# Four raw buffers for heads 0 to 7, loaded three heads ahead

## The chip, the cores and the metric

The kernel runs on one core of one Trainium2 chip. The time is that of one execution on the device, in microseconds (us); several runs are made and their median counts. A profile is one more execution, recorded instruction by instruction. Engines: TensorE (PE; its weight loads are PEld), VectorE (DVE), ScalarE (ACT), GpSimd (POOL), SyncE (SP). SP computes nothing here, it issues nearly all DMAs; a few are issued from ScalarE's queue (ACTq).

## The reference

Batch 4, 8 heads, 576 positions, head size 64; 32 heads in all. Weights come in float64.

```python
# attention, each of the 32 heads
cum = cumsum(maximum(s, 0))
scores = q @ k.T / 8 + minimum(-(cum[:, None] - cum[None, :]), 0)   # causal
attn = softmax(scores)                     # minus the row's maximum, sum + 1e-9
x = attn @ v                               # to [batch, 576, 512]
# first mixing
gate = sigmoid(causal_conv5(x, conv_w))
x = (gate * (x @ w_val)) @ w_out
# second mixing
u, v = split(relu(x @ w_in), 2)            # 512 columns each
v = layernorm(v)
out = (u * (w_spatial @ v + b_spatial)) @ w_out2
```

## The kernel before, in words

One loop goes over the heads, w = 0 to 32. Step w computes the scores of head w in five row tiles (of 64, 128, 128, 128 and 128 rows; the last in two pieces, so six pieces), and for head w-1 the transposes of the exponentials. VectorE reads each score piece out of PSUM, adds the mask and takes the row's extremum (line 233); ScalarE takes the exponential with its row sum (line 238); TensorE transposes (line 279), ScalarE copies the transposes to `pt` (line 281). Two heads make a pair: `normalise` takes the reciprocals of a pair's row sums, `lay_sums` stores them from ScalarE's queue into `r_d` in DRAM, `spread_sums` loads them back, spread over 64 partitions, as `R` in two halves (line 262). `pv` multiplies by v for a pair (line 303), and VectorE multiplies its result by `R` to `x` (lines 306 to 309). `conv` then makes the gate `z`.

The scores of heads 0 to 7 (NATIVE = 8) are plain float32 matmuls on the raw q and k tile (line 222); a row of ones and a row of `cum` in partition 64 bring in the bias. From head 8 on the raw tile is split by `prep` into a high and a low part (tiles `qk`, `kd`, `cn`), and a score piece is two faster matmuls (lines 224 and 225).

`load(h)` brings head h in: three DMAs into the raw tile, for heads 0 to 7 one more for the row of `cum` (from the tile for heads 0 and 1, from its copy `one_d` in DRAM for the others), and two into `vraw` (v, four buffers in turn). So a load is five or six issues on SP. There are two raw tiles, `RAW[0]` and `RAW[1]`; head h uses `RAW[h % 2]`, so the load of head h waits until the scores of head h-2 are done (heads 0 to 7), or its split (later ones). `vraw` of head h takes the buffer of head h-4 and waits for that head's `pv`. `qk` has two buffers as well, unused until head 8.

Beside the heads runs the work of a generator, a piece after each group of score tiles (`more`). In the first heads it converts float64 weights, chunk by chunk (`from_f64`): conv_w, four chunks of woT, four of w_in, four of w_val, four more of w_in, then w_out2. A chunk is one load on SP (line 382), one instruction on ScalarE (384), three on VectorE (385 to 387), two on GpSimd (390, 391), and a split in two. Then TensorE folds w_out into w_in (`fold`), and from step 9 on does the mixing of batch 0, later of the others, between the scores.

A scheduler orders the instructions of every engine by their place in the program and by when it expects operands and buffers. The orders are fixed when the kernel is built, and every engine, and SP's queue, works through its own in turn.

Of the kernel before, what the change touches and what calls it, by code (L numbers as in the profile page):

```python
# [8 lines left out]
F32R = mybir.dt.float32r  # L9
# [7 lines left out]
NATIVE = 8  # L17
# [7 lines left out]
def tile_stickbreak_attention_moe(  # L25
# [18 lines left out]
    NH, S = s.shape  # L44
# [20 lines left out]
    V, G, A, T, SY = nc.vector, nc.gpsimd, nc.scalar, nc.tensor, nc.sync  # L65

    def f(ap):
        return ap.bitcast(F32)
# [13 lines left out]
    early = ctx.enter_context(tc.tile_pool(name="early", bufs=1))  # L82
# [8 lines left out]
    RAW = [early.tile([128, 2, S], F32, name=f"raw{i}") for i in range(2)]  # L91
# [36 lines left out]
    for j in range(2):  # L128
        P.append(early.tile([128, PW], F32, name=f"p{j}"))
        G.memset(P[j][64:, 192:256], 0.0)  # L130
        G.memset(P[j][:, 576:640], 0.0)
    mid = ctx.enter_context(tc.tile_pool(name="mid", bufs=1))

    def tmp(name, dt=F32):
# [8 lines left out]
    raw, vraw, L = {}, {}, {}  # L143
# [4 lines left out]
    def load(h, cum=None):  # L148
        if h >= NH:
            return  # L150
        raw[h] = r = RAW[h % 2]
        n = 64 if h < NATIVE else 128
        src = qk2[h].rearrange("p (t s) -> p t s", t=2)[0:n, ::-1]
        by = r[0:n].rearrange("p t s -> p (t s)")
        SY.dma_start(by[:, 64:1088].rearrange("p (t s) -> p t s", t=2)[:, :, 0:448], src[:, :, 0:448])
        by = by.rearrange("p (g c) -> p g c", c=64)
        SY.dma_start(by[:, 0:17:16], src[:, :, 512:])
        SY.dma_start(by[:, 8:18:9], src[:, :, 448:512])
        if h < NATIVE:
            SY.dma_start(r[64:65, 0, :], one_d[h:h + 1] if cum is None else cum[h:h + 1])  # L160
        vraw[h] = early.tile([128, 6, D], F32, tag="vraw", name="vraw", bufs=4)
        vh = vp[h].rearrange("p (c d) -> p c d", c=5)
        SY.dma_start(vraw[h][:, 0:4], vh[:, 0:4])
        SY.dma_start(vraw[h][64:128, 4:], vh[0:64, 0::4])
# [78 lines left out]
    def normalise(p):  # L243

        d = early.tile([128, 2, 5], F32, tag="den", name="den", bufs=2)
        V.tensor_scalar_add(d, sm[p % 2], 1e-9)
        R[p] = early.tile([128, 2, 5], F32, tag="rin", name="rin", bufs=2)
        V.reciprocal(out=R[p], in_=d)
# [22 lines left out]
    def transposes(h, tiles):  # L271

        p = P[h % 2]
        if h not in PT:
            PT[h] = early.tile([128, PTW], F32, tag="pt", name="pt", bufs=2)
        for bank in tiles:
            pt = room("t", "pst", h)
            for t, (o, way) in enumerate(BANKS[bank]):
                T.transpose(pt[:, 128 * t:128 * t + 128], p[:, o:o + 128], ident[:, way:way + 128])  # L279
            to, o, n = PTO[bank]  # L280
            A.activation(PT[h][:, to:to + n], pt[:, o:o + n], AF.Copy)  # L281
# [3 lines left out]
    def pv(h):  # L285

        b, p = h // H, (h % H) // 2
        x = X[b, p] = early.tile([128, S], F32, tag=f"x{p}", name=f"x{p}", bufs=1)
        r = R.pop(h // 2)
        pts = [PT.pop(h + j) for j in range(2)]  # L290
        vs = [vraw.pop(h + j) for j in range(2)]
        po = ps.tile([128, 512], F32, tag="o", name="pso", bufs=1)
        pq = ps.tile([128, 512], F32, tag="q", name="psq", bufs=1)[:, 0:64]
        parts = [(0, 0, po), (2, 1024, po[:, 192:]), (3, 1408, po[:, 320:]), (4, 1344, po[:, 448:]),
                 (1, 576, po[:, 64:]), (5, 512, pq)]
        first = None
        for c, o, to in parts:
            k0 = 64 if c > 3 else 0
            for j in (1, 0):
                with ExitStack() as es:  # L300
                    if first is not None:
                        es.enter_context(tc.issue_after(first))
                    m = T.matmul(to[64 * j:64 * j + 64], vs[j][k0:, 4 + (c == 4) if c > 3 else c, :],  # L303
                                 pts[j][k0:, o:o + to.shape[1]], start=c in (0, 5), stop=c in (1, 5))
                first = first or m.ins
        V.tensor_tensor(out=x[:, 64:448], in0=po[:, 0:384], in1=r[:, 1:4].rearrange("p i q -> p (i q)"), op=ALU.mult)
        xs, ps4, r4 = [t.rearrange("p (g c) -> p g c", g=2) for t in (x[:, 448:], po[:, 384:], r[:, 4])]
        V.tensor_tensor(out=xs, in0=ps4, in1=r4[:, ::-1], op=ALU.mult)
        V.tensor_tensor(out=x[:, 0:64], in0=pq, in1=r[:, 0, 0:64], op=ALU.mult)
# [3 lines left out]
    def conv(b, p):  # L313
        x = X[b, p]
        if p == 0:
            Z[b] = early.tile([128, NP, S], F32, tag="z", name="z", bufs=1)
        z = Z[b][:, p, :]
        A.activation(z, x, AF.Copy, scale=cw[:, p, 4:5])  # L318
        for k in range(3, -1, -1):
            d = 4 - k  # L320
            V.scalar_tensor_tensor(out=z[:, d:], in0=x[:, :S - d], scalar=cw[:, p, k:k + 1], in1=z[:, d:],  # L321
                                   op0=ALU.mult, op1=ALU.add)
        A.activation(z, z, AF.Tanh)
# [16 lines left out]
    if NATIVE:  # L340
        load(0, cum)
        load(1, cum)
        SY.dma_start(one_d, cum[0:NATIVE])
    if not NATIVE:
        load(0)
        load(1)
# [164 lines left out]
    def mixing_a(b):  # L511

        xh, xl = [], []
        for p in KC:
            xh.append(mid.tile([128, S], F32R, tag=f"xvh{p}", name=f"xvh{p}"))
            xl.append(mid.tile([128, S], F32R, tag=f"xvl{p}", name=f"xvl{p}"))
            hi_of(A, xh[p], X[b, p])
            lo_of(V, xl[p], X[b, p], xh[p])
        z = Z[b]
        g = GT[b] = mid.tile([128, NP, 2 * S + 64], F32R, tag="g", name="g")  # L520
        gh, gl = g[:, :, 0:S], g[:, :, S + 64:]
        for mc in KC:
            wh, wl = weight_chunk(wv_d, mc, b)
            for hf in range(2):
                pt = ps.tile([128, 512], F32, tag="m", name="psm", bufs=2)
                three(pt[:, 0:HS], KC, lambda kc: (wh[:, kc, :], wl[:, kc, :]),
                      lambda kc: (xh[kc][:, hs[hf]], xl[kc][:, hs[hf]]))
                gated_split(gh[:, mc, hs[hf]], gl[:, mc, hs[hf]], pt[:, 0:HS], z[:, mc, hs[hf]], 1.0)
                yield 1.44
# [87 lines left out]
    def more(n):  # L617
        with tc.high_priority(offset=0):
            more_(n)
# [42 lines left out]
    def start():  # L662

        m = mixing_a(0)
        yield from both(m, first, 2)
        m = mixing_b(0)
        yield from both((next(m) for _ in range(5)), second_steps())
        for ec in range(4):
            fold(ec, 0)
            yield 2.56  # L670
        open_late()
        yield from both((next(m) for _ in range(8)), third_steps())
        yield from m
# [14 lines left out]
    for w in range(NH + 1):  # L688
        if w == H + 1:
            queue.clear()  # L690
            queue.append(start())
        elif w % H == 1 and w > 1 and w < NH:
            queue += [mixing_a(w // H - 1), mixing_b(w // H - 1)]
        if w >= NATIVE:
            load(w + 2)
        n_g = [3, 11.5, 10.0, 7.6, 6.0][0 if w <= H else 1 if w <= H + 4 else 2 if w <= 2 * H else 3 if w <= 3 * H else 4]
        gs = [n_g / 5] * 5
        if w < NH:
            scores(w, [0, 1])
        if w > H + 1 and w % 2:  # L700
            pv(w - 3)
            conv((w - 3) // H, ((w - 3) % H) // 2)
        if w > 0:
            transposes(w - 1, [3, 2])
        if w % 2 == 0 and w > 0:
            lay_sums(w // 2 - 1)
        more(gs[0])
        if w < NH:
            scores(w, [2])
        prep(w + 1)  # L710
        if 0 < w <= H:
            transposes(w - 1, [0])
        more(gs[1])
        if w < NH:
            scores(w, [3])
        if w > 0:
            transposes(w - 1, [0, 1] if w > H else [1])
        if w % 2 == 0 and w > 0:
            spread_sums(w // 2 - 1)
        more(gs[2])  # L720
        if w < NH:
            scores(w, [4])
            if w < NATIVE:
                load(w + 2)
            if w % 2:
                normalise(w // 2)
        more(gs[3])
        if w % 2 == 0 and (0 < w <= H or w == NH):
            pv(w - 2)
            conv((w - 2) // H, ((w - 2) % H) // 2)  # L730
        more(gs[4])
# [57 lines left out]
```

## Time and profile before

| | us |
|---|---|
| median of 3 runs | 505.13 |
| lowest, highest | 504.92, 505.87 |
| the profiled execution | 505.84 |
| its span, first to last instruction | 504.1 |
| TensorE busy in the span | 478.4 |
| VectorE, ScalarE, GpSimd busy | 320.0, 315.8, 166.6 |

The span is 1.7 us shorter than the time of the same execution, and that time is 0.7 us above the median. Busy shares of the span are averages over stages which differ, so the views below go by stretches of time.

### The profile page before, as it was taken

To read this page: it belongs to the slowest core of one execution; us is meant where nothing else is said; L and a number is where in the kernel's file an instruction comes from. 1 tells how busy PE (TensorE), PEld (TensorE's weight loads), DVE (VectorE), ACT (ScalarE), POOL (GpSimd) and SP (SyncE) were. 2 spreads that over 40 slices of the span, in tenths; PEclk is the share of its full clock that TensorE was granted. 3 is DMA by queue.
4 is the path that set the end of the run, shared out by engine and by line. 5 is a ranking of instruction groups with operands and counts; after the bars stand their busy time and mean duration, and the time that the engine had idled before them with its cause. 6 is when DMAs were issued, how large, how long until landed. Compare 5 with 4: busy or idle time off the path is not lost.

```text
span 504.1 us, 9144 instructions
## 1 busy us (share of the span) xinstructions
PE 478.4 (95%) x3138; PEld 402.7 (80%) x3138; DVE 320.0 (63%) x835; ACT 315.8 (63%) x796; POOL 166.6 (33%) x183
## 2 busy tenths in 40 slices
PE   8787889899899999998999999999999999999997
PEld 5443556678777899996969889898878979988997
DVE  5799999598989783742768366654885534124120
ACT  2887876787776875773667657585778524234322
POOL 5697252056583103101353013002243023136130
PEclk9999799989999999999999999999999999999999
DMA  3877466557493634377631413677611072700002
GB/s 92 255 232 241 133 209 223 156 159 236 122 270 121 185 106 123 99 212 191 186 87 42 130 39 85 187 217 200 169 37 32 0 262 53 225 1 2 0 11 85
DMA packets 51567, 68.23 MB, mean 135 GB/s; under 512 B 23936, under 2 KB 39456, under 8 KB 51520
## 3 DMA queue, kind: packets, MB, share of 16 engines
q1 hardware_dynamic: 46592, 62.84, 42.6%
q10 hardware_dynamic: 4928, 4.80, 2.8%
q8 instruction: 25, 0.41, 0.4%
q14 instruction: 22, 0.18, 0.1%
HBM read 54.91 MB, written 9.16 MB: 127 GB/s over the span
## 4 chain that ended last, share of the span: by engine, by line
PE 65%; DVE 17%; DMA 9%; ACT 3%; issue 3%; SPq 2%; POOL 1%; DVEq 0%; ACTq 0%; POOLq 0%
PE psm L426 12%; PE psm L428 11%; PE psm L427 11%; PE pso L303 6%; PE pst L279 5%; PE psm L594 4%; PE psm L596 3%; PE psm L595 3%; DVE p L233 3%; PE pss L224 3%; PE pss L225 3%; DVE z L321 3%; DMA raw<-in_qk 2%; DMA wv<-wv_d 2%; DMA R<-r_d 2%
## 5 line engine op out<-in xcount | busy, mean ns | idle before, releaser
L238 ACT ACTIVATE p<-p,nm 64x64 f32<-64x64 f32 (+4 forms) x160 | 88.5, 554 | 20.4 <-DVE nm L233 19.9
L233 DVE CUSTOM_DVE_ANT_0 p<-pss,mask 64x64 f32<-64x64 f32 (+4 forms) x160 | 62.8, 413 | 24.1 <-PE pss L225 18.4
L281 ACT ACTIVATE pt<-pst 128x512 f32<-128x512 f32 (+2 forms) x128 | 59.5, 496 | 21.4 <-PE pst L279 20.7
L279 PE MATMUL pst<-ident,p 128*128 128x128 f32 x416 | 64.5, 281 | 1.3 <-ACT p L238 1.2
L80 POOL TENSOR_TENSOR y<-gt,y 128x288 fp32r<-128x288 f32 x32 | 27.9, 872 | 106.6 <-ACT y L73 106.6
L80 POOL TENSOR_TENSOR g<-gt,g 128x288 fp32r<-128x288 f32 x32 | 28.2, 886 | 96.2 <-ACT g L73 96.0
L321 DVE SCALAR_TENSOR_TENSOR z<-x,cw,z 128x575 f32<-128x575 f32 (+1 forms) x64 | 56.1, 876 | 6.3 <-ACT z L318 5.8
L279 PEld LDWEIGHTS pst<-ident,p 128*128 128x128 f32 x416 | 50.7, 144 | 10.7 <-issue 3.4
L303 PE MATMUL pso<-pt,vraw 128*64 128x512 f32 (+4 forms) x320 | 52.6, 437 | 0.0
L224 PE MATMUL pss<-qk 128*64 128x64 f32 (+1 forms) x144 | 44.0, 324 | 3.3 <-DVE nm L233 3.0
L225 PE MATMUL pss<-kd,cn 66*64 66x64 f32 (+1 forms) x144 | 41.8, 296 | 0.0
L504 DVE TENSOR_TENSOR gt<-psm,u 128x288 f32<-128x288 f32 x32 | 14.5, 455 | 43.0 <-PE psm L598 33.3
L222 PE MATMUL pss<-raw 128*128 128x320 f32 (+4 forms) x96 | 31.8, 437 | 8.6 <-DVE nm L233 5.6
L426 PE MATMUL psm<-g,wch 128*128 128x288 f32 x128 | 38.7, 302 | 0.9 <-DVE wcl L80 0.9
L594 PE MATMUL psm<-wsh,vh 128*128 128x288 f32 x128 | 38.5, 304 | 0.4 <-DVE gt L504 0.4
L428 PE MATMUL psm<-g,wch 128*128 128x288 f32 x128 | 38.1, 297 | 0.0
L427 PE MATMUL psm<-g,wcl 128*128 128x288 f32 x128 | 38.0, 297 | 0.0
L596 PE MATMUL psm<-wsl,vh 128*128 128x288 f32 x128 | 37.5, 297 | 0.0
L595 PE MATMUL psm<-wsh,vl 128*128 128x288 f32 x128 | 37.3, 296 | 0.0
L303 PEld LDWEIGHTS pso<-pt,vraw 128*64 128x64 f32 (+1 forms) x320 | 19.0, 135 | 22.6 <-issue 15.4
L502 DVE SCALAR_TENSOR_TENSOR gt<-z,psm 128x288 f32<-128x288 f32 x32 | 14.2, 449 | 35.5 <-PE psm L428 35.4
L426 PE MATMUL psm<-xvh,wv 128*128 128x288 f32 x96 | 29.7, 309 | 2.9 <-DMA wv<-wv_d 2.4
(168 smaller groups left out, 1345.2 us busy)
## 6 DMA issues: line engine op xcount, KB each, us to landing
raw<-in_qk SPq DMA_DIRECT2D x24, 448.0 KB
wv<-wo_d SPq DMA_DIRECT2D x12, 512.0 KB
R<-r_d SPq DMA_DIRECT2D x32, 160.0 KB
wv<-wv_d SPq DMA_DIRECT2D x10, 512.0 KB
out<-ot ACTq DMA_DIRECT2D x32, 144.0 KB
vraw<-in_vp SPq DMA_DIRECT2D x32, 128.0 KB
cn<-qk SPq DMA_DIRECT2D x24, 144.0 KB
raw<-in_qk SPq DMA_DIRECT2D x48, 64.0 KB
```

The source lines that it names most:

```text
L224: T.matmul(pst[0:m, o:o + b - a], qa[:, q0:q0 + m], kb[:, k0 + a:k0 + b], start=True, stop=False)
L225: T.matmul(pst[0:m, o:o + b - a], qc[0:KD, q0:q0 + m], kd[0:KD, k0 + a:k0 + b], start=False, stop=True)
L233: LAST["V"] = V.tensor_tensor_reduce(out=row[:, a:b], in0=src, in1=mask[0:m, o:o + b - a], scale=-0.125, scalar=3.0e38 if a == 0 else nm[0 ...
L238: A.activation(row, row, AF.Exp, bias=nm[0:m, i:i + 1], scale=-1.0, accum_out=sm[h // 2 % 2][0:m, h % 2, i:i + 1])
L279: T.transpose(pt[:, 128 * t:128 * t + 128], p[:, o:o + 128], ident[:, way:way + 128])
L281: A.activation(PT[h][:, to:to + n], pt[:, o:o + n], AF.Copy)
L303: m = T.matmul(to[64 * j:64 * j + 64], vs[j][k0:, 4 + (c == 4) if c > 3 else c, :], pts[j][k0:, o:o + to.shape[1]], start=c in (0, 5), sto ...
L321: V.scalar_tensor_tensor(out=z[:, d:], in0=x[:, :S - d], scalar=cw[:, p, k:k + 1], in1=z[:, d:], op0=ALU.mult, op1=ALU.add)
L426: T.matmul(pt, ah, bh, start=j == 0, stop=False)
L427: T.matmul(pt, al, bh, start=False, stop=False)
L428: T.matmul(pt, ah, bl, start=False, stop=j == n - 1)
L594: T.matmul(o, vh[c][:, cs], wsh[:, c, hs[hf]], start=c == 0, stop=False)
```

## The change

Heads 0 to 7 now use four raw tiles in turn: the two old ones and two allocated under the tag `qk`, whose two buffers are later those of the split tiles. Their constant rows are set by GpSimd, two memsets for each. Head 2 is loaded ahead of the loop; in the loop step w loads head w+3 for w = 0 to 6, where it loaded head w+2 for w = 0 to 7. From head 10 on the loads stand as before. `vraw` still has four buffers.

```diff
--- before.py
+++ after.py
@@ -129,6 +129,11 @@
         P.append(early.tile([128, PW], F32, name=f"p{j}"))
         G.memset(P[j][64:, 192:256], 0.0)
         G.memset(P[j][:, 576:640], 0.0)
+    for i in range(2):
+        t = f(early.tile([128, 2, S], F32R, tag="qk", name="rawq", bufs=2))
+        G.memset(t[64:], 0.0)
+        G.memset(t[64:65, 1, :], 1.0)
+        RAW.append(t)
     mid = ctx.enter_context(tc.tile_pool(name="mid", bufs=1))
 
     def tmp(name, dt=F32):
@@ -148,7 +153,7 @@
     def load(h, cum=None):
         if h >= NH:
             return
-        raw[h] = r = RAW[h % 2]
+        raw[h] = r = RAW[h % (4 if h < NATIVE else 2)]
         n = 64 if h < NATIVE else 128
         src = qk2[h].rearrange("p (t s) -> p t s", t=2)[0:n, ::-1]
         by = r[0:n].rearrange("p t s -> p (t s)")
@@ -341,6 +346,7 @@
         load(0, cum)
         load(1, cum)
         SY.dma_start(one_d, cum[0:NATIVE])
+        load(2)
     if not NATIVE:
         load(0)
         load(1)
@@ -720,8 +726,8 @@
         more(gs[2])
         if w < NH:
             scores(w, [4])
-            if w < NATIVE:
-                load(w + 2)
+            if w + 1 < NATIVE:
+                load(w + 3)
             if w % 2:
                 normalise(w // 2)
         more(gs[3])
```

The lines below the edits move by 5, 6 further down (line 155 becomes 160, line 262 becomes 267, line 382 becomes 388).

The first place is SP's queue behind the loads of heads 0 and 1. `raw_66` and `raw_67` are the two old tiles, `rawq` the new ones. Before, from the store of one_d to the end of head 2's raw load:

```order
L343 DMA one_d<-cum 8x576
L347 DMA cum_d<-ch 32x576
L348 DMA cum_d<-cl 32x576
L382 DMA wg<-in_conv_w 128x40
L382 DMA wg<-in_woT 128x1024
L163 DMA vraw<-in_vp 128x256
L164 DMA vraw<-in_vp 64x2x64
L382 DMA wg<-in_woT 128x1024
L155 DMA raw_66<-in_qk 64x2x448
L157 DMA raw_66<-in_qk 64x2x64
L158 DMA raw_66<-in_qk 64x2x64
L160 DMA raw_66<-one_d 1x576
```

And with the change:

```order
L348 DMA one_d<-cum 8x576
L160 DMA rawq<-in_qk 64x2x448
L162 DMA rawq<-in_qk 64x2x64
L163 DMA rawq<-in_qk 64x2x64
L165 DMA rawq<-one_d 1x576
L168 DMA vraw<-in_vp 128x256
L169 DMA vraw<-in_vp 64x2x64
L353 DMA cum_d<-ch 32x576
L354 DMA cum_d<-cl 32x576
L388 DMA wg<-in_conv_w 128x40
L388 DMA wg<-in_woT 128x1024
L160 DMA rawq<-in_qk 64x2x448
```

Head 2's six issues have moved from behind conv_w and two woT chunks to right behind one_d; cum_d, conv_w and woT stand behind them, and head 3's raw load follows the first woT chunk.

The second place is SP's queue around R of pair 0. Before, from the last woT chunk; the raw load is head 4's:

```order
L382 DMA wr<-in_woT 128x1024
L382 DMA wg<-in_w_in 128x1024 x2
L180 DMA kd_117<-cum_d 2x576
L155 DMA raw_66<-in_qk 64x2x448
L157 DMA raw_66<-in_qk 64x2x64
L158 DMA raw_66<-in_qk 64x2x64
L160 DMA raw_66<-one_d 1x576
L382 DMA wg<-in_w_in 128x1024
L180 DMA kd_118<-cum_d 2x576
L382 DMA wr<-in_w_in 128x1024
L262 DMA R<-r_d 64x640 x2
L163 DMA vraw<-in_vp 128x256
```

And with the change, from the last woT chunk; the raw load is head 5's, the vraw loads are those of heads 4 and 5:

```order
L388 DMA wr<-in_woT 128x1024
L160 DMA raw_67<-in_qk 64x2x448
L162 DMA raw_67<-in_qk 64x2x64
L163 DMA raw_67<-in_qk 64x2x64
L165 DMA raw_67<-one_d 1x576
L267 DMA R<-r_d 64x640
L168 DMA vraw<-in_vp 128x256
L169 DMA vraw<-in_vp 64x2x64
L267 DMA R<-r_d 64x640
L168 DMA vraw<-in_vp 128x256
L169 DMA vraw<-in_vp 64x2x64
L388 DMA wg<-in_w_in 128x1024 x2
```

R stood in one piece behind the four w_in chunks and ahead of vraw; now the vraw load of head 4 stands between its halves and the w_in chunks behind both.

The third place is SP's queue around R of pair 1. Before; the raw load is head 6's:

```order
L382 DMA wg<-in_w_val 128x1024 x3
L155 DMA raw_66<-in_qk 64x2x448
L157 DMA raw_66<-in_qk 64x2x64
L262 DMA R<-r_d 64x640 x2
L158 DMA raw_66<-in_qk 64x2x64
L160 DMA raw_66<-one_d 1x576
L163 DMA vraw<-in_vp 128x256
L164 DMA vraw<-in_vp 64x2x64
L163 DMA vraw<-in_vp 128x256
L164 DMA vraw<-in_vp 64x2x64
```

And with the change; the raw load is head 8's, the vraw loads are those of heads 6 and 7:

```order
L388 DMA wr<-in_w_val 128x1024
L160 DMA raw_66<-in_qk 128x2x448
L162 DMA raw_66<-in_qk 128x2x64
L163 DMA raw_66<-in_qk 128x2x64
L185 DMA kd_117<-cum_d 2x576
L185 DMA kd_118<-cum_d 2x576
L168 DMA vraw<-in_vp 128x256
L169 DMA vraw<-in_vp 64x2x64
L267 DMA R<-r_d 64x640 x2
L168 DMA vraw<-in_vp 128x256
L169 DMA vraw<-in_vp 64x2x64
```

R of pair 1 stood ahead of both vraw loads; now it stands between them, behind that of head 6.

## Rows read from the trace of the kernel before

**Rows 1.** The page, part 1: busy us of each engine, share of the span, instructions.

```profile
PE 478.4 (95%) x3138; PEld 402.7 (80%) x3138; DVE 320.0 (63%) x835; ACT 315.8 (63%) x796; POOL 166.6 (33%) x183
```

**Rows 2.** Stretches (us): length, then busy us (instructions) by engine, granted clock, DMA share, GB/s.

```profile
8.00:25.00 17.00, 13.05 (x63) 8.26 (x64) 10.67 (x47) 12.19 (x39) 7.67 (x8) 1.00 0.75 208
25.00:85.00 60.00, 51.64 (x260) 32.13 (x261) 58.07 (x147) 46.42 (x117) 35.66 (x24) 0.94 0.68 215
85.00:100.00 15.00, 13.51 (x87) 9.90 (x85) 9.55 (x28) 11.81 (x33) 0.00 (x0) 1.00 0.54 147
100.00:137.50 37.50, 34.57 (x209) 28.93 (x210) 35.67 (x88) 29.11 (x74) 20.24 (x16) 0.95 0.56 170
137.50:504.10 366.60, 359.11 (x2505) 318.62 (x2503) 200.62 (x517) 214.26 (x535) 96.14 (x117) 1.00 0.40 116
```

**Rows 3.** TensorE's waits to 140 us: line, releaser, us in total, times, longest.

```profile
PE pss L222 <- DVE nm L233: 5.6, 7, 1.0
PE pss L224 <- DVE nm L233: 3.0, 2, 2.6
```

**Rows 4.** VectorE by line, 20 to 60 us: count, busy us, mean ns of one.

```profile
L387 DVE SCALAR_TENSOR_TENSOR wg<-wg 128x512 int32<-128x512 int32 x4 | 3.4, 861 | 0.0
L386 DVE TENSOR_SCALAR wg<-wg 128x512 int32<-128x512 int32 x5 | 3.4, 676 | 0.0
...
L385 DVE TENSOR_SCALAR wg<-wg 128x512 f32<-128x512 f32 x5 | 2.8, 561 | 0.0
```

**Rows 5.** SP's queue in order of time: start us, us of the issue, line.

```profile
10.70 0.32 SPq L347 DMA_DIRECT2D cum_d<-ch  x1
...
12.49 0.43 SPq L163 DMA_DIRECT2D vraw<-in_vp  x1
12.96 0.60 SPq L164 DMA_DIRECT2D vraw<-in_vp  x1
13.61 0.59 SPq L382 DMA_DIRECT2D wg<-in_woT  x1
14.30 0.60 SPq L155 DMA_DIRECT2D raw<-in_qk  x1
14.95 0.60 SPq L157 DMA_DIRECT2D raw<-in_qk  x1
15.59 0.61 SPq L158 DMA_DIRECT2D raw<-in_qk  x1
16.24 0.45 SPq L160 DMA_DIRECT2D raw<-one_d  x1
```

**Rows 6.** Timeline near the first loads: start us, us, work, [idle before and what ended it].

```profile
13.39 0.22 ACT L384 ACTIVATE wg<-wg 128x20 f32<-128x20 f32 x1 [2.46 <-DMA wg<-in_conv_w]
...
19.05 1.55 POOL L390 TENSOR_SCALAR wg<-wg 128x512 int32<-128x512 uint32 x1 [1.76 <-DMA wg<-in_woT]
...
20.37 0.82 PE L222 MATMUL pss<-raw 128*64 128x64 f32 x4 [2.33 <-DMA raw<-in_qk]
```

**Rows 7.** VectorE's waits from 8 to 140 us, columns as in rows 3.

```profile
DVE x L306 <- DMA R<-r_d: 3.0, 2, 2.2
DVE wg L385 <- ACT wg L384: 1.8, 1, 1.8
```

**Rows 8.** Timeline: sums of pair 0 stored, R loaded; R of pair 3, its use.

```profile
28.18 0.56 ACTq L256 DMA_DIRECT2D r_d<-rt  x1
...
33.04 1.12 SPq L262 DMA_DIRECT2D R<-r_d  x2
...
94.86 1.11 SPq L262 DMA_DIRECT2D R<-r_d  x2
...
99.04 0.56 DVE L306 TENSOR_TENSOR x<-pso,R 128x384 f32<-128x384 f32 x1 [2.22 <-DMA R<-r_d]
```

**Rows 9.** GpSimd by line to 9 us, columns as in rows 4.

```profile
L94 POOL MEMSET raw<- 64x1152 f32 x1 | 1.1, 1052 | 0.3 <-POOLq L774 0.3
```

**Rows 10.** One more stretch, columns as in rows 2.

```profile
101.00:105.00 4.00, 3.88 (x16) 3.34 (x17) 3.97 (x12) 3.96 (x12) 2.12 (x1) 0.58 0.17 37
```

## The prediction

> **What bounds the kernel now.** I read the page's busy shares first: TensorE is busy 478.4 of 504.1 us [rows 1], so the whole change can only play for the 26 us in which TensorE is idle, and for stretches in which its clock is low. The table by stage says where these lie [rows 2]. Behind 137.5 us TensorE is busy 359.1 of 366.6 us: nothing that loads heads 0 to 8 earlier shortens that stage. Between 8 and 137.5 us it is busy 112.8 of 129.5 us, so 16.7 us are idle there: 4.0 before 25 us, 8.4 from 25 to 85, 1.5 to 100 and 2.9 to 137.5.
>
> What ends these waits? Mostly VectorE: the score matmuls wait 5.6 us in seven pieces (heads 0 to 7) and 3.0 us in two (from head 8 on) until VectorE has read an earlier score tile [rows 3]. VectorE is the bound from 25 to 85 us, busy 58.07 of 60 us, because it converts the float64 weights between the score tiles. A weight chunk costs it three instructions of 0.56, 0.68 and 0.86 us, 2.1 us together [rows 4]. So in that stage a wait is worth something only if it is a wait of VectorE, and VectorE's own waits are few: 1.9 us. Before 25 us it idles 6.3 of 17 us and from 85 to 100 us 5.4 of 15 us [rows 2]. The change must earn its gain in these two places, and must not make a new wait in between.
>
> **The change part by part.** The arithmetic is the same; two pairs of memsets are new, no load is added, and the loads and everything else are put in another order.
>
> (a) *Head 2 no longer waits for head 0's buffer.* TensorE waits 2.33 us for its raw tile, whose first load is issued at 14.30 us [rows 5, 6]. Now it is issued right behind one_d, where cum_d stood, some 3.6 us earlier. Gain 2.3 us; bounds 0 (something else holds VectorE at that place) and 2.3.
>
> (b) *conv_w.* The load of head 2 is six issues (0.60, 0.60, 0.61, 0.45, 0.43 and 0.60 us, sum 3.3 us [rows 5]) put ahead of cum_d, conv_w and the first woT chunk. Now VectorE waits 1.8 us for conv_w's conversion [rows 7]; ScalarE begins that at 13.39 us, when the load has landed [rows 6]. Landing moves to 16.7 us. In the new order VectorE meets this conversion behind the fifth score tile of head 1 instead of behind the fifth of head 0, at about 16 us by the old times less the old wait. So 1.8 us go and about 0.6 come back: gain 1.2, bounds 0.9 and 1.8.
>
> (c) *woT later.* The second woT chunk was issued at 13.61 us and GpSimd began on it at 19.05 us, 5.4 us later [rows 5, 6]. Now head 2's load (3.3 us) and head 3's raw tile (0.60, 0.60, 0.61, 0.45: 2.3 us) stand ahead of it: issue 19.2, landing about 24.6 us. VectorE wants it behind the last tile of head 2, which with (a) and (b) gained it reaches at about 23.4 us. Loss 1.2 us; bounds 0 and 2.
>
> (d) *R of pair 0 behind a vraw load.* The vraw buffers are still four, so the load of head w+3 waits for pv of head w-1, an iteration earlier than before. On SP's queue the first vraw load of head 4 now stands between the two halves of R, and of head 5 right behind; the two w_in chunks that stood ahead of R now stand behind all of these. R's halves were issued at 33.04 us, 4.9 us after r_d [rows 8]. r_d moves up with head 2 by 1.5 to 2 us, so R's first half goes out at about 30 to 31.5 us; one half (0.56), two vraw issues (0.43 and 0.60) and the other half (0.56) end 2.2 us later; another pair of halves took 99.04 - 94.86 - 1.11 = 3.1 us from the last issue to the multiply that waited for it [rows 8]. R is there at 35.3 to 36.8 us. VectorE comes to the multiply (x, line 306) earlier than before, for two w_in chunks, 4.2 us [rows 4], are no longer ahead of it: at 32 to 33 us. It then stands for 2 to 4 us, and what is queued behind x on VectorE is the last tile of head 3, which TensorE's next score matmuls wait for. Loss 3 us; bounds 2 and 4.
>
> [...] In the trace SP's queue is served strictly in its order: no row of it starts before the one ahead [rows 5]. [...]
>
> (e) *R of pair 1* stands in the same way behind vraw of head 6 (before: ahead of it). VectorE is saturated there, so I take less: loss 1 us; bounds 0 and 2.7 (the 2.2 us that R's second half is held up in (d), and 0.5 for the last matmuls of pv, which I estimate).
>
> (f) *The memsets.* GpSimd gets two of 64x1152 (1.05 us each [rows 9]) and two of one row, which I take at no more than half a wide one each, ahead of its last masks: the masks come some 2 to 3 us later. They were done before the first score tile needs them; most is covered by that slack. Loss 0.3 us; bounds 0 and 0.5. Without that cover it would be the whole 3.2.
>
> (g) *Heads 8 to 10.* The raw tile of head 9 was issued behind w_val and pair 2; now it is loaded an iteration earlier, so the split of heads 9 and 10 is no longer late. [...] TensorE is otherwise full here, and the new order also puts mixing matmuls ahead of head 8's third tile, so a wait saved is kept. [...]
>
> Behind 137.5 us the order differs up to head 28, but TensorE has 7.5 us idle there in all; I take 0, with 1 us to either side.
>
> **The sum.** -2.3 - 1.2 + 1.2 + 3 + 1 + 0.3 - 3.5 = -1.5 us. The profiled execution took 505.84 us (span 504.1 and 1.7 around it), 0.7 above the median of 505.13. Against its own time that is 504.3, against the median **503.6 us**, 0.3% faster. With every bound at its best: -2.3 - 1.8 + 0 + 2 + 0 + 0 - 4.7 - 1 = -7.8; at its worst: 0 - 0.9 + 2 + 4 + 2.7 + 0.5 + 0 + 1 = +9.3.
>
> **The rivals.** What a measurement of this kernel can tell from no change is about 0.2%, 1.0 us.
>
> *Slower: SP's queue blocks.* R of pairs 0, 1 and 2 is stuck behind vraw loads that wait for pv, and the weight loads behind R with it. Place: x <- R on VectorE between 32 and 76 us. Price: 4 + 2.7 + 2 for pair 2 (as pair 3 before, 2.2), 8.7 us, against gains of 2.3 + 1.2 and losses of 1.2 + 0.3 in (b), (c), (f), and half of (g), 2.4: net +4.3, 509.4 at full price; it decides from about 5.5 us of such waits on (2.3 + 1.2 - 1.5 + 3.5, the point of no change) and counts as slower from 6.5. For it: the order, in which vraw stands ahead of R for both pairs. Against: pv(0) is issued early in head 3, so vraw may find it done. Chance 0.33; about 507 as its middle. [...]
>
> *No change.* VectorE's work up to head 8 is the same sum, and it has but 1.9 us idle from 25 to 85 us; heads that come earlier only trade places with weights that come later, and (g) is lost to R of pair 3 once more. Time 505.1, chance 0.21. For it: the nearly equal busy sums. Against: the two idle places are outside that stage.
>
> *Much faster.* vraw finds pv done, (d) and (e) cost 1 together, (g) is whole: -2.3 - 1.2 + 1.2 + 1 + 0.3 - 4.7 = -5.7, 499.4 us; chance 0.14.
>
> *The change does not do what it says.* Head 2's row of cum comes from one_d in DRAM, written just ahead; if that round trip and the full queue bring head 2 as late as before, (a) is nothing and (b), (c) and (d) stay: about +1 us, 506. It is within the two rivals above.
>
> **Chances.** My forecast (501.5 to 504.1) has 0.32; with the much faster case, faster by over 0.2% is 0.46, within 0.2% 0.21, slower 0.33. The likeliest case's own range is 501.5 to 504.5. To hold eight in ten the range goes from the much faster case, 499.5, to 508.0, which leaves out the slower rival's full price and the best sum.
>
> **What would show it.** (a) No wait of a score matmul for raw, head 2's first matmul near 16 us instead of 20.37. (b), (c) Waits of ScalarE on conv_w and woT. (d), (e) Waits of x (line 311 then) on R between 32 and 60 us, of 2 to 4 and 0 to 2.7 us; SP's queue waiting on pv in front of vraw. (g) No low clock near 101 us, less than 1 us of waits of the score matmuls of heads 8 to 10. I am wrong if the waits on R in that stage come to more than 6 us, or if the waits at heads 8 to 10 are as long as before.

## The result, and the profile after

The changed kernel takes 511.2 us (median of four runs, 509.1 to 512.6), the kernel before 505.0 us beside it: ratio 1.0129, 95% interval 1.0095 to 1.0163, 6.2 us slower. The forecast was 503.6 us. The profiled execution after took 512.62 us, with a span of 510.8; before it was 505.84 and 504.1.

The stages of the changed kernel, in the columns of [rows 2]:

```profile
8.00:25.00 17.00, 14.94 (x74) 9.25 (x76) 9.97 (x46) 12.51 (x41) 6.29 (x14) 1.00 0.67 185
25.00:85.00 60.00, 47.77 (x228) 27.73 (x224) 55.68 (x135) 44.17 (x110) 38.97 (x25) 0.91 0.67 206
85.00:100.00 15.00, 14.41 (x70) 10.53 (x70) 10.58 (x31) 9.36 (x25) 2.06 (x1) 0.81 0.49 148
100.00:137.50 37.50, 34.35 (x227) 28.79 (x226) 36.08 (x83) 28.12 (x72) 23.87 (x16) 1.00 0.65 187
137.50:504.10 366.60, 359.92 (x2503) 318.00 (x2502) 203.81 (x532) 216.81 (x547) 96.61 (x116) 1.00 0.39 115
504.10:510.80 6.70, 3.60 (x28) 3.37 (x26) 0.00 (x0) 1.23 (x3) 0.00 (x0) 0.98 0.28 88
```

Take length less TensorE's busy time in each row, and subtract the same from [rows 2]: 1.9 us of idle time are saved before 25 us, 3.9 are added from 25 to 85, 0.9 saved to 100, 0.2 added to 137.5, 0.8 saved behind it, and 3.1 stand in the last row: 3.6 us more in all, 2.3 of them behind 137.5 us. The clock: 0.09 x 60 + 0.19 x 15 = 8.3 us of work lost, against 0.06 x 60 + 0.05 x 37.5 = 5.5 before: 2.8 more. Together they are 6.4 of the 6.7 us by which the span grew. So the gain at the start arrived, and the stage that was VectorE's (58.07 us busy before, 55.68 now) gave it back twice over; the 2.3 us behind 137.5 lie scattered (the most from 150 to 200 us, where TensorE idles 2.3 us instead of 0.9), and no run says what made them.

What SP's queue did (first line: head 2's raw tile; columns of [rows 5]):

```profile
10.66 0.60 SPq L160 DMA_DIRECT2D rawq<-in_qk  x1
...
15.26 0.42 SPq L388 DMA_DIRECT2D wg<-in_conv_w  x1
...
19.68 0.59 SPq L388 DMA_DIRECT2D wg<-in_woT  x1
...
30.73 0.47 SPq L267 DMA_DIRECT2D R<-r_d  x1
...
34.49 1.01 SPq L388 DMA_DIRECT2D wg<-in_w_in  x2
...
54.60 0.54 SPq L388 DMA_DIRECT2D wg<-in_w_val  x1
```

Three rows of the kernel before that were not shown ahead say when the same chunks went out there:

```profile
11.53 0.42 SPq L382 DMA_DIRECT2D wg<-in_conv_w  x1
...
22.49 0.84 SPq L382 DMA_DIRECT2D wg<-in_w_in  x2
...
40.01 4.13 SPq L382 DMA_DIRECT2D wg<-in_w_val  x3
```

conv_w is 3.7 us later, woT's second chunk 6.1, the first of four w_in chunks 12.0 (the others 10.6 to 12), the first of four w_val chunks 3.6 and the other three 14 to 17. Part of the last is a wait of the queue itself: it stood 4.0 us in front of head 6's values until `pv` was done, and R of pair 1 and the three w_val chunks went out behind them (R at 52.01 us, 47.24 before). The waits of VectorE and ScalarE from 8 to 140 us answer to the lateness (columns of [rows 3]):

```profile
DVE wil L80 <- ACT wih L73: 4.2, 2, 2.5
...
DVE wg L391 <- ACT wg L390: 2.3, 3, 1.0
DVE wa L391 <- ACT wa L390: 2.1, 2, 1.3
...
DVE x L311 <- DMA R<-r_d: 0.9, 2, 0.8
```

```profile
ACT wa L390 <- DMA wr<-in_woT: 2.9, 1, 2.9
ACT wa L390 <- DMA wr<-in_w_in: 2.4, 2, 1.8
ACT wg L390 <- DMA wg<-in_conv_w: 1.5, 1, 1.5
```

VectorE now stands 4.4 us for the first step of a conversion, 1.8 before [rows 7], but only 0.9 us for R, 3.0 before. It also stands 4.2 us for ScalarE's half of a split (`wih`), 1.8 of them at 54.92 us, for a w_in chunk that GpSimd had finished late. The dearest place comes later. First the changed kernel, then the kernel before, from 80 to 91 us (columns of [rows 2]):

```profile
80.00:91.00 11.00, 8.24 (x28) 6.35 (x28) 9.98 (x23) 3.91 (x11) 3.10 (x2) 0.69 0.70 229
```

```profile
80.00:91.00 11.00, 10.39 (x60) 6.71 (x59) 9.64 (x26) 7.64 (x19) 0.00 (x0) 1.00 0.63 198
```

TensorE idles 2.8 us instead of 0.6, and by its granted clock 0.31 x 11 = 3.4 us are lost. VectorE still splits the last two w_val chunks here, at 80.80 and 84.20 us; before, it did so at 77.09 and 80.16. GpSimd's 3.1 us (before 0) are further w_in chunks. What TensorE waits for stands right behind such a split on VectorE:

```profile
80.80 1.49 DVE L80 TENSOR_TENSOR wg<-wg 128x512 fp32r<-128x512 f32 x1
82.21 0.67 DVE L80 TENSOR_TENSOR wcl<-psm,wch 128x512 fp32r<-128x512 f32 x1
...
82.94 0.40 PE L432 MATMUL psm<-xvh,wv 128*128 128x288 f32 x1 [1.42 <-DVE wcl L80]
```

### The profile page after: what moved, and what is told of

Read it like the earlier page. It is cut to its first block, busy times and chain, and to the rows that moved or that the text cites. A ratio compares the mean times of both kernels' runs of the same rounds, so it can differ in the third digit from the quotient of the medians.

```text
span 510.8 us, 9147 instructions
## 1 busy us (share of the span) xinstructions
PE 481.2 (94%) x3138; PEld 402.3 (79%) x3138; DVE 321.4 (63%) x835; ACT 314.2 (61%) x796; POOL 174.9 (34%) x187
## 4 chain that ended last, share of the span: by engine, by line
PE 56%; DVE 4%; DMA 4%; ACT 3%; issue 1%; POOL 1%; SPq 1%; ACTq 0%; DVEq 0%; POOLq 0%
PE psm L432 10%; PE psm L434 9%; PE psm L433 9%; PE pso L308 6%; PE pst L284 4%; PE psm L600 3%; PE psm L601 3%; PE psm L602 3%; PE pss L229 2%; PE pss L230 2%; DMA wv<-wo_d 2%; DMA out<-ot 1%; DVE z L326 1%; DMA wsr<-in_wsT 1%; PE psm L603 1%
## 5 line engine op out<-in xcount | busy, mean ns | idle before, releaser
L284 PE MATMUL pst<-ident,p 128*128 128x128 f32 x416 | 65.8, 280 | 6.2 <-ACT p L243 4.3
L80 POOL TENSOR_TENSOR y<-gt,y 128x288 fp32r<-128x288 f32 x32 | 29.2, 917 | 113.0 <-ACT y L73 112.8
L80 POOL TENSOR_TENSOR g<-gt,g 128x288 fp32r<-128x288 f32 x32 | 29.5, 927 | 89.5 <-ACT g L73 86.3
L308 PE MATMUL pso<-pt,vraw 128*64 128x512 f32 (+4 forms) x320 | 51.2, 437 | 0.1
L615 ACT ACTIVATE ot<-psm 128x288 f32<-128x288 f32 x32 | 12.9, 410 | 33.1 <-PE psm L434 25.8
L432 PE MATMUL psm<-y,wv 128*128 128x288 f32 x96 | 29.3, 306 | 2.8 <-DMA wv<-wo_d 1.9
```

The costliest lines, as they stand in the source:

```text
L80: eng.tensor_tensor(out=out_, in0=in_, in1=f(hi), op=ALU.subtract)
L432: T.matmul(pt, ah, bh, start=j == 0, stop=False)
```

## Experiments

Each was timed over five rounds beside the kernel before on the same chip; ratios are to it, with 95% intervals. The theory followed through them is called 1, W or Q as it was sharpened: weights that come late on SP's queue.

**Parts of the change undone, the scheduler ordering everything anew.** e1: raw tiles early, values at the old place.

```diff
+        if h > 1 and h < NATIVE + 2:
+            return
+        load_v(h)
+
+    def load_v(h):
         vraw[h] = early.tile([128, 6, D], F32, tag="vraw", name="vraw", bufs=4)
...
                 load(w + 3)
+            if w < NATIVE:
+                load_v(w + 2)
```

> The changed kernel, but only the raw tiles are loaded three heads ahead; the loads of the values (vraw) stand where they stood before the change, two heads ahead. Theory 1 (weights late: the weight chunks w_in and w_val come onto SP's queue 12 to 15 us later than before, behind raw loads and behind R's wait for r_d, and their conversion piles up later): the three-ahead raw loads and R still stand ahead of the chunks, so most of the loss stays, 508 to 512 us. Theory 2 (SP's queue stands 4.0 us in front of vraw of head 6, waiting for pv, and that holds up everything): that wait shrinks and the time comes back to 504 to 506. Theory 3 (no one place, the whole order is another one): nothing definite, 506 to 512.

Measured 505.5 us, 1.0019 (1.0000 to 1.0039): the values make the difference, as theory 2 had it, though w_in (31.6 us) and w_val (from 54.4) went out nearly as late as in the changed kernel. There the last two w_val chunks are split at 79.02 and 80.40 us all the same, and from 80 to 91 us TensorE is busy 10.15 us at full clock. So late weights alone do not decide: how late their conversion comes out hangs on the engines' order too.

e2: only head 2 early, the others two heads ahead.

```diff
-            if w + 1 < NATIVE:
-                load(w + 3)
+            if 0 < w < NATIVE:
+                load(w + 2)
```

> The changed kernel with its four buffers and its early load of head 2, but heads 3 to 9 are loaded two heads ahead again. Theory 1 (weights late): two w_in chunks stand ahead of R of pair 0 again and three w_val chunks ahead of R of pair 1, so most of the loss is gone and head 2's gain of 2 us stays, 502.5 to 505.5. Theory 2 (pv wait): values are loaded as before, so no wait for pv, 502.5 to 505. Theory 3 (the whole order): 505 to 511.

508.0 us, 1.0067 (1.0041 to 1.0094), slower than theories 1 and 2 had it: in the order that the scheduler makes of them, four buffers and an early head 2 cost more than they bring.

e3: the kernel before, with six weight chunks held back, three of w_in and three of w_val (the expectation says seven).

```diff
-        SY.dma_start(r, src.rearrange("p (c t) -> p c t", t=2))
+        with ExitStack() as es:
+            if 6 <= count[0] <= 13 and count[0] not in (9, 10) and "R" in LAST:
+                es.enter_context(tc.issue_after(LAST["R"].ins))
+            SY.dma_start(r, src.rearrange("p (c t) -> p c t", t=2))
```

> The kernel before, with nothing of the change, but seven weight chunks are held back on SP's queue: the first three of w_in behind R of pair 0, three of w_val behind R of pair 1 (as they stand after the change). Theory 1 (weights late): slower than before by most of what the change costs, 508 to 512 us, with the low clock and the idle TensorE moved to between 75 and 95 us. Theory 2 (pv wait): no wait for pv is added, so 504 to 506. Theory 3: 504 to 510.

508.6 us, 1.0092 (1.0058 to 1.0126), as theory 1 said. With late weights, and without any part of the change, most of its loss is there (w_in goes out at 32.6 us, three w_val chunks from 61.3); but here too the scheduler ordered everything anew.

e4: the first fourteen weight loads from ScalarE's queue.

```diff
-        SY.dma_start(r, src.rearrange("p (c t) -> p c t", t=2))
+        (A if count[0] <= 14 else SY).dma_start(r, src.rearrange("p (c t) -> p c t", t=2))
```

> The changed kernel, but the loads of conv_w and of the first twelve weight chunks are issued from ScalarE's queue instead of SP's, so that neither raw nor vraw nor R stands ahead of them. Theory 1 (weights late): the chunks come early again and the loss goes, 501 to 506 us. Theory 2 (pv wait): SP's queue still stands in front of vraw of head 6 and R of pair 1 behind it, so 508 to 511. Theory 3: 505 to 511. Both 1 and 2 allow some loss from ScalarE's standing at an issue.

509.4 us, 1.0104 (1.0074 to 1.0134). It tells little: woT's loads now go out from 1.2 us on, beside head 0's and 1's, and VectorE begins on head 0's first tile at 12.5 us instead of 9.1.

**Which values?** e5 puts those of heads 2 and 3 back, e6 those of heads 4 to 9; e7 writes head 2's load behind conv_w; e8 is e7 with all values at the old place.

e5:

```diff
+        if 1 < h < 4:
+            return
...
+            if w < 2:
+                load_v(w + 2)
```

> The changed kernel, but the values (vraw) of heads 2 and 3 alone are loaded at their old places; those of heads 4 to 9 stay three heads ahead. Theory 1a (first weights late: the values of heads 2 and 3 stand ahead of conv_w and woT on SP's queue, and VectorE waits 3.6 us for ScalarE's first step of their conversion between 17 and 32 us, 0.7 us where the values stand behind): most of the loss goes, 504.5 to 506.5 us. Theory 2 (values of heads 4 to 7 stand ahead of the weights, split R's halves and wait for pv): the loss stays, 509 to 511. Theory 3 (any edit gives another order of all engines, and that decides): no relation, 505 to 511.

e6:

```diff
+        if 4 <= h < NATIVE + 2:
+            return
...
+            if 1 < w < NATIVE:
+                load_v(w + 2)
```

> The counterpart: the values of heads 4 to 9 are loaded at their old places, those of heads 2 and 3 three heads ahead as after the change. Theory 1a (first weights late): the loss stays, 509 to 511 us, with VectorE's waits for the first step of the conversion of 3 us or more before 32 us. Theory 2 (values of heads 4 to 7): the loss goes, 504.5 to 506.5. Theory 3: no relation, 505 to 511.

e7, and e8 with e1's edit besides:

```diff
-        load(2)
...
         more(gs[0])
+        if w == 0:
+            load(2)
```

> The changed kernel, but the early load of head 2 is written behind conv_w's and woT's first chunk in the program; everything later is as changed. Theory 1a (first weights late): VectorE's waits for the first conversions shrink to 1 to 2 us, 505 to 508 us. Theory 2 (values of heads 4 to 7): the loss stays, 509 to 511. Theory 3: 505 to 511.

> All values at their old places and the early load of head 2 behind conv_w and woT's first chunk; raw tiles three heads ahead. Theory 1a (first weights late): the best of these, 502.5 to 505 us. Theory 2: as with the values alone at their old places, 504.5 to 506.5. Theory 3: 504 to 510.

e5 509.6 us (1.0080, 1.0053 to 1.0107), e6 516.7 (1.0203, 1.0161 to 1.0246), e7 511.9 (1.0118, 1.0084 to 1.0151), e8 509.3 (1.0072, 1.0049 to 1.0096). The two halves of e1's edit do not add up: against the changed kernel's ratio of 1.0129 one gains 0.5%, the other loses 0.7%, both together gain 1.1%. Neither 1a nor 2 as a sum of parts can be right: e5 came out where 2 had it, and e6, e7 and e8 above both. Every edit lets the scheduler write another order for all engines, so these runs can't price a single load.

**The order held.** An edge without a wait between neighbours of a written list makes each compute engine run in the order of the list. The lists were read from the two kernels. e9: loads of the change, order of before; e10 crosswise; e11 and e12: e1 and e2 in the order of before.

```diff
     while queue:
         more(1)
+    hold_order(tc)
...
+def hold_order(tc):
...
+        for a, b in zip(order, order[1:]):
+            tc.add_manual_dep(mine[b], mine[a].name,
+                              mybir.DependencyInfo(mybir.DependencyClass.NoSync, mybir.DependencyReason.DATA),
+                              reason="hold_order")
```

> The changed kernel (four buffers, memsets, early load of head 2, loads three heads ahead), but TensorE, VectorE, ScalarE and GpSimd run their instructions in the order of the kernel before, row for row; only SP's queue is ordered anew. Theory Q (queue: the loss is made by loads and weights that wait in SP's queue): it stays, 509 to 512 us. Theory O (order: the loss is made by the order that the scheduler wrote for the four compute engines when it took the loads for earlier): it goes, 502 to 505.5 us, and head 2's gain may show.

> The crosswise one: buffers and loads of the kernel before, but the four compute engines run in the order of the changed kernel, row for row. Theory Q (queue): 504 to 506.5 us, for the loads are where they were. Theory O (order): 508 to 513 us, the changed kernel's time without any of its loads.

> Raw tiles three heads ahead in four buffers, values at their old places, compute engines in the order of the kernel before. Theory Q: as with its own order, 504.5 to 506.5 us. Theory O: 502 to 505 us, no worse than before, since no wait of the old order is lengthened but for conv_w's and woT's.

> Four buffers, head 2 early, the others two heads ahead, compute engines in the order of the kernel before. Theory Q: as with its own order, 507 to 509 us. Theory O: 502 to 505 us.

e9 512.4 us (1.0153, 1.0112 to 1.0195), e10 519.9 (1.0302, 1.0267 to 1.0336), e11 509.1 (1.0093, 1.0059 to 1.0127), e12 508.7 (1.0068, 1.0034 to 1.0101). With the old order the loss stays, as theory Q said for e9 (0.4 us above its range) and e12: the loads make it without the new order. e11 came out slower than either theory, and so did e10: the new order without its loads is worse still. It wants raw tiles early, TensorE waits 3.7 us and ScalarE 11.5 us for them, and three w_val chunks go out at 59.7 us; so e10 does not show what the order costs by itself. e9's waits from 8 to 140 us, of ScalarE and of TensorE:

```profile
ACT wg L390 <- DMA wg<-in_conv_w: 6.2, 1, 6.2
...
ACT wg L390 <- DMA wg<-in_w_val: 3.4, 1, 3.4
```

```profile
PE pst L284 <- ACT p L243: 13.8, 4, 5.0
```

ScalarE stands at a weight that has not landed, the exponentials behind it are late, and TensorE's transposes wait for them: 8.6 of the 13.8 us right behind these two stands (4.96 at 18.08 us, 3.62 at 65.65). Another 4.58 us (at 47.13) follow a stand of ScalarE that the profile puts on VectorE, which had itself stood 1.75 us for R. So not all of it is weights. And it is not the changed kernel's place: in e9 more is lost before 25 us (1.2 us of idle time and 3.4 of clock more than before) and from 25 to 85, and from 80 to 91 us TensorE is as full as before (10.77 us, clock 1.00).

**One lateness at a time.** e13: only four w_in chunks and w_val's four from ScalarE's queue, own order; e14: e7 in the old order; e15: four buffers alone, loads written as before, old order; e16: e13's edit on e1.

e13 and e16:

```diff
-        SY.dma_start(r, src.rearrange("p (c t) -> p c t", t=2))
+        (A if 5 < count[0] <= 13 else SY).dma_start(r, src.rearrange("p (c t) -> p c t", t=2))
```

e15:

```diff
-        load(2)
...
-            if w + 1 < NATIVE:
-                load(w + 3)
+            if w < NATIVE:
+                load(w + 2)
```

> The changed kernel in its own order, but the eight chunks of w_in and w_val that are loaded between 34 and 58 us are issued from ScalarE's queue, so that neither R's wait nor raw nor vraw loads stand ahead of them; conv_w and woT stay on SP's queue. Theory W (the loss is made where the late chunks are converted, in heads 7 and 8, where TensorE's idle time and low clock grow by 6 us): 504.5 to 507.5 us, and no more than 1 us of additional idle time between heads 7 and 8. Theory S (the loss is made at the start, by conv_w and woT that come 3.7 us late, and only shows later): 509 to 513 us.

> Loads as changed, compute engines in the order of the kernel before, but the load of head 2 is written behind conv_w's, so that cum_d, one piece of head 2 and then conv_w stand on SP's queue. Theory S (start): VectorE's wait for conv_w, 5.6 us when head 2 stood ahead of it in this order, falls to 2 to 3 us, and the time with it, from 512.4 to 508.5 to 510. Theory W: the start doesn't matter, 511 to 514.

> Four buffers, all loads written where they were before the change, compute engines in the order of the kernel before. On SP's queue conv_w and woT's first chunk stay ahead, head 2's tile comes right behind them, and w_in and w_val stay ahead of R nearly as before. Theories S and W both: nothing is late, and the 2.3 us that TensorE waits for head 2 shrink, 502 to 505 us. If the memsets or the full queue cost something of their own: 505 to 508.

> Raw tiles three heads ahead, values at their old places, w_in and w_val issued from ScalarE's queue, own order. Theory W: better than with the chunks on SP's queue (505.5 us), 501.5 to 504.5. Theory S: no better, 505 to 508, since conv_w is as late as there.

e13 took 514.5 us (1.0195, 1.0160 to 1.0230), e14 512.8 (1.0156, 1.0121 to 1.0191), e15 510.1 (1.0095, 1.0061 to 1.0129), e16 515.0 (1.0198, 1.0167 to 1.0229). Of the forecasts of totals only W's for e14 held; e13, e15 and e16 came out above both theories. In e14 VectorE's wait for conv_w falls from 5.6 to 3.6 us, and the time stays. e13's stages (columns of [rows 2]):

```profile
25.00:45.00 20.00, 13.40 (x62) 7.54 (x57) 15.88 (x42) 12.76 (x33) 15.31 (x12) 0.83 0.80 215
...
80.00:91.00 11.00, 10.00 (x53) 8.19 (x52) 10.69 (x26) 8.15 (x20) 5.22 (x4) 1.00 0.79 248
```

From 80 to 91 us TensorE is nearly as busy as before and at full clock, as W says for that place. But ScalarE's queue is no free queue: from 26 to 46 us ScalarE waits 5.4 us for w_in, and TensorE idles 6.6 of 20 us. In e15 the first 15 us are as before (the first tile of head 1, conv_w's wait); woT's second chunk and three w_in chunks then come 1 to 2.4 us late, and the fourth much later. SP's queue, then ScalarE:

```profile
28.66 0.33 SPq L387 DMA_DIRECT2D wg<-in_w_in  x1
29.43 0.60 SPq L160 DMA_DIRECT2D rawq<-in_qk  x1
33.87 1.12 SPq L267 DMA_DIRECT2D R<-r_d  x2
...
39.50 0.33 SPq L387 DMA_DIRECT2D wr<-in_w_in  x1
```

```profile
43.86 0.66 ACT L389 ACTIVATE wa<-wr 128x512 f32<-128x512 f32 x1 [6.87 <-DMA wr<-in_w_in]
```

The fourth w_in chunk has slipped behind R, in front of which nothing goes out from 30.03 to 33.87 us, and behind seven more loads: out at 39.50 instead of 30.81 us. ScalarE stands 6.87 us at it, and what is behind it with it: TensorE's transposes wait up to 7.4 us for an exponential in this run. What the prediction took in (d), that a wait of the queue holds up the loads behind it, is what such rows show: in the changed kernel too the queue stands 2.5 us for the sums in front of R's first half (30.73 us) and 4.0 us for `pv` (50.89 us), and nothing behind goes out meanwhile.

**The weights keep their places.** All buffers and memsets of the change, but SP's queue in its old order, except for three moves meant for places where the queue has nothing to lose: woT's second chunk and head 2's tile ahead of head 2's values, the raw tiles of heads 5 and 7 ahead of a wait. e17 holds the compute engines to the old order too, as e9 does; e18 leaves them to the scheduler and has SP's list alone.

```diff
 ORDER = {
...
+    'SP': ...
 }
```

> Buffers and memsets of the changed kernel, compute engines in the order of the kernel before, and SP's queue in its old order too, but for three moves: woT's second chunk and head 2's raw tile go ahead of head 2's values, and the raw tiles of heads 5 and 7 go ahead of a wait of the queue. No weight chunk and no R stands behind a load that it didn't stand behind before, except woT by head 2. Theory Q (loads that wait for no buffer any more push the weights back, and the compute engines, which keep their order, stand for them): nothing is late, head 2's wait of 2.3 us shrinks by 1 to 2 us, ScalarE waits less than 1 us for w_in, 502 to 504.8 us. Rival (four buffers, memsets or fuller DMA rings cost something by themselves): 506 to 510.

> The same order of SP's queue, but the scheduler writes the order of the compute engines itself, knowing when the weights come. Theory Q: about the same, 501.5 to 505 us. Rival (the scheduler's own order is what costs): 507 to 512, as the changed kernel.

e17 takes 505.7 us, 1.0006 (0.9978 to 1.0034): the loss is gone, the gain that I expected is not there. e18 takes 507.2 us, 1.0046 (1.0019 to 1.0074), not what theory Q had (501.5 to 505) but at the lower edge of its rival, by which the scheduler's own order costs. e9 and e17 have the same buffers, memsets and compute order, row for row; only the order of SP's queue differs, and it makes the difference between 1.0153 and 1.0006. With the scheduler free, the same queue takes the changed kernel from 1.0129 to 1.0046, and the intervals do not meet. What these pairs show is the price of the queue's order as a whole: raw tiles, values and R are back in their old places along with the weights, and no run puts back the weights alone on SP's queue. SP's queue in e9, then in e17:

```profile
15.25 0.43 SPq L388 DMA_DIRECT2D wg<-in_conv_w  x1
...
39.31 1.12 SPq L267 DMA_DIRECT2D R<-r_d  x2
40.53 0.54 SPq L388 DMA_DIRECT2D wr<-in_w_in  x1
```

```profile
11.55 0.42 SPq L388 DMA_DIRECT2D wg<-in_conv_w  x1
...
33.97 0.36 SPq L388 DMA_DIRECT2D wr<-in_w_in  x1
34.38 1.12 SPq L267 DMA_DIRECT2D R<-r_d  x2
```

Why does e17 not gain, with head 2 early? Its TensorE and VectorE:

```profile
18.88 0.82 PE L227 MATMUL pss<-rawq 128*64 128x64 f32 x4 [0.87 <-DMA rawq<-one_d]
```

```profile
39.64 0.56 DVE L311 TENSOR_TENSOR x<-pso,R 128x384 f32<-128x384 f32 x1 [3.33 <-DMA R<-r_d]
```

Head 2 begins 1.5 us earlier than before (20.37 us, [rows 6]). VectorE reaches x of pair 0 at 36.31 us, 1.1 earlier than before (37.41, without a wait), and then stands 3.33 us for R. R goes out at 34.38 us, 1.3 later than before (33.04 us, [rows 8]): head 5's raw tile was moved ahead of the fourth w_in chunk, which leaves at 33.97 instead of 30.81 us, and R behind it. So one of the three moves did cost something, and against the expectation (under 1 us) ScalarE waits 4.8 us for w_in. No run beat the kernel before; e1 and e17 can't be told from it.

## Why the prediction was wrong

**Right.** (a) Head 2's first matmul begins at 16.53 us instead of 20.37, near the 16 I named, and none of its score matmuls waits for its tile. (f) The memsets cost nothing that shows: VectorE's first score tile starts at 9.14 us, 9.25 before, though it now waits for GpSimd's mask there (1.5 us), so the slack is used up. Of (g) two signs came: the low clock at 101 us is gone (granted clock 1.00 from 101 to 105), and VectorE's waits for R fall from 3.0 to 0.9 us.

**Wrong: the step in (d) that moved two w_in chunks behind R.** I used it only to let VectorE reach x earlier, "for two w_in chunks, 4.2 us, are no longer ahead of it", and gave their own lateness no price. All four w_in chunks moved, by 10.6 to 12 us, and three of w_val by 14 to 17, and engines that work in order stood for them (ScalarE 2.4 us for w_in chunks). The work did not vanish: the last of it fell into 80 to 91 us, where TensorE then idled and ran slowly. That is the largest missing term, about 2.2 us of idle time and 3.4 of clock at that one place. e9 against e17 shows that with the compute order held the queue's order makes the whole loss, the changed kernel against e18 that it makes about two thirds with the order free. That the weights are the part of the queue that counts is argued from the waits and from e3 (0.9%), and e1 sets a bound to it: weights nearly as late, and no loss clear of the noise.

**Wrong in size: (b), (c) and (g).** (b) and (c) summed to 0. VectorE's waits for the first conversion step, which I expected to come to 0.6 us at conv_w and 1.2 at woT, are 1.0 and 2.7 us, the second outside its bounds. In e9, where the order can't give way, ScalarE's wait for conv_w alone is 6.2 us. (g) was to bring 3.5 us, three quarters of 4.7. No run shows these 4.7 us as one loss: the kernel before has 3.0 us of VectorE's waits for R [rows 7], 3.0 of TensorE's on VectorE from head 8 on [rows 3], and a clock of 0.58 for 4 us, 1.7 us of work [rows 10]. From 85 to 137.5 us TensorE idles 0.7 us less, but loses 2.9 us by its clock where it lost 1.9: nothing is gained. Score matmuls from head 8 on still wait 1.8 us (under 1 was expected), and the low clock has moved ahead, to 85 to 91 us. Behind 137.5 us I took 0, with 1 us to either side; in the profile it is 2.3 us of idle time.

**Wrong in place: (d) and (e).** Waits for R of 3 + 1 us were expected and 0.9 came. R was there when I said (x starts at 35.85 us), but VectorE came 2 to 3 us later than I said, held up by the weights (at 31.19 us it has stood 1.34 us for a woT chunk). In e17, where VectorE comes earlier, it waits 3.33 us for R, which there goes out later as well.

**The rivals.** The slower one had the sign and its queue, and not its place: the queue did stand for `pv` in front of head 6's values, 4.0 us, but I put the price on x waiting for R between 32 and 76 us. "[A]nd the weight loads behind R with it" stood in its sentence, without a price. The range ended at 508.0, short of that rival's full 509.4. And neither of the two signs by which I would have known that I was wrong appeared: both looked at R and at heads 8 to 10.

**What stays open.** Why neighbours like e1 (505.5 us) and e6 (516.7 us) lie 11 us apart. Each has its own order of all engines and its own stretches of low clock (e1 has a mean of 0.83 from 25 to 85 us, and still equals the kernel before), and no run tells these two apart. Open too is what the 0.46% of e18 is made of, and how the price of the queue's order divides among weights, R and the rest.

## What to carry to other kernels

Before a load is moved ahead on a full queue, list every transfer that it passes and every wait of the queue that these now stand behind, and price each at the engine that meets it in order; a buffer that never makes the queue wait is not free if it lets a load pass what is needed sooner (e15, the buffers alone: 0.95%). Where a scheduler orders all engines, hold its order fixed to price a single edit: with the order free, the parts of one edit did not add up here (0.5% and -0.7%, together 1.1%). Before a gain at the head of a chain is counted, look at what the chain waits for next: in e17 head 2 began 1.5 us earlier, and VectorE then stood 3.33 us for R, which had not moved up as well.

## What was not expected of the hardware

Single executions of one and the same kernel lie far apart: 501.2 to 508.3 us for the kernel before in the last session, 503.2 to 509.1 for e17. In the changed kernel the granted clock falls close behind a stretch in which TensorE has little to do. Two such pairs:

```profile
50.00:53.00 3.00, 1.58 (x9) 0.63 (x7) 3.00 (x8) 2.63 (x9) 2.92 (x2) 1.00 0.21 54
53.00:63.50 10.50, 9.14 (x24) 5.21 (x25) 8.40 (x24) 7.98 (x20) 7.65 (x8) 0.51 0.84 286
...
80.00:85.40 5.40, 2.64 (x15) 1.92 (x14) 5.40 (x11) 2.29 (x6) 1.04 (x1) 0.86 0.67 212
85.40:91.00 5.60, 5.60 (x14) 4.43 (x15) 4.58 (x13) 1.62 (x6) 2.06 (x1) 0.53 0.73 245
```

TensorE is busy 1.58 of 3.0 us and then gets about half its clock (0.51) for 10.5 us; 2.64 of 5.4 us, and again (0.53) for 5.6 us. That is 1.4 us of idle time with 0.49 x 10.5 = 5.1 us of lost clock behind it, and 2.8 us with 0.47 x 5.6 = 2.6. The kernel before has the first pair too (busy 1.63 us from 50 to 53, then a granted clock of 0.67 to 63.5); the second it has not (4.79 of 5.4 us busy, and 1.00 behind). That the idle stretch brings the low clock is what these pairs suggest; no run was made to show it.
